# A fused attention and two-MoE kernel on one core: another place for the short token block, and low parts on VectorE

## The chip, the cores and the metric

The kernel runs on one core of one Trainium2 chip. The metric is the device time of one execution in microseconds (us). TensorE is called PE here, VectorE DVE, ScalarE ACT, GpSimd POOL; PEld is the weight load that stands ahead of each matmul, and SP is the engine that issues the DMAs.

## What is computed

Multi-head attention with a threshold under the row maximum, then two dense two-layer stages ("MoE" and "MoE 2"), all in float32. The change touches the second one alone (`_moe2_ref`):

```python
x = np.ascontiguousarray(attn_out.transpose(0, 2, 1, 3)).reshape(B * S, H * D)   # 2304 x 512
x = _moe_ref(x=x, **moe_kwargs)

def _moe2_ref(x, w_in, w_out):        # x 2304 x 512, w_in 512 x 2048, w_out 2048 x 512
    h = x @ w_in
    g = h * (1.0 / (1.0 + np.exp(-1.702 * h)))
    return g @ w_out
```

## The kernel before, in words

**Split products.** Every factor of a product is kept as a high and a low part (fp32r). The high part is a rounding copy made by ACT; the low part is source minus high part, a two-input subtraction on DVE or POOL. A product is three matmuls: high x high, high x low, low x high.

**The second MoE** walks over the tokens in blocks: four full ones of 512 tokens (first tokens 0, 512, 1024, 1536) and a short one of 256 (first token 2048; `BLOCKS`, L351). It does so twice, once for each half of the 2048 hidden units, eight units of 128 columns in a half, taken in four pairs. The first pass stores its result to DRAM (`y2d`), the second adds to it and writes the output. Before, the first pass goes short, 0, 512, 1024, 1536, and the second 0, 512, 1024, 1536, short.

**A block** (`moe2`, L922) has three steps. `halves` (L814) loads the block's inputs in two halves of the model dimension (tiles xa and xb, one buffer each) and makes the left factors from them: seven for a full block, which multiplies two-by-two blocks with seven products instead of eight, and two for the short block. A full block needs four subtractions first (xt, xa, xb written; called XD here). Each factor i is then a copy on ACT (outhring, called XHC) and a subtraction of 128 x 512 (outlring, called XLC) on the engine `XENG[i]` (L353): before, POOL for factors 0, 2, 4 and 6, DVE for 1, 3 and 5. The factors live in a ring of eight buffers. `hidden2` (L871) makes the hidden values of a pair: seven products (six matmuls of 256 columns each) for a full block, four for a short one, with ACT copies (p, u, c) and DVE additions (c) that take results out of PSUM, four banks (pm) in all. `gate2` (L858) applies the gate to each unit of the pair: a sigmoid on ACT (tc), a product on DVE (tc), the high part on ACT (g) and the low part (g, called GL here) on the engine that `hidden2` hands it: before, POOL for the first unit of a pair and DVE for the second, and DVE for both in a block's last pair. `yout` then multiplies both units into four accumulators (py): 24 matmuls of 512 columns for a pair of a full block, of 256 for the short one.

**Beside the first blocks** other work runs on the same engines: the int64-coded weights of the last pair of the first half are decoded, and those of the second half, which are stored (kept) for the second pass. A decode is ACT, DVE and POOL work on tiles wrstg, wmstg and ws, and high and low parts inhring, inlring, outhring, outlring (ring1) again.

**What sets the order.** Nothing is written in program order: a planner places every operation by a due time and a table of costs, and each engine then runs its own list in that order. So an operation that waits holds back all that stands behind it on its engine. The tiles xa and xb live in memory that the first MoE's inputs hold (`change2`, L1016), so the first loads of the second MoE go out only after the last hidden product of the first.

Of the kernel before, what the change touches and what calls it, by code (L numbers as in the profile page):

```python
# [21 lines left out]
PE, ACT, DVE, POOL, SP, DMA = range(6)  # L22
# [220 lines left out]
def tile_top_attention_moe_moe2(  # L243
# [52 lines left out]
    def add(eng, cost, time, name, fn, rd=(), wr=(), touch=()):  # L296
        op = pl.add(eng, cost, time, fn, rd, wr, name, touch)
        for c, names in zip(changed, (LATE, LAST)):
            if any(b.pool in names for b in op.bufs):
                op.deps.add(c)  # L300
        return op
# [14 lines left out]
    def mark():  # L316
        return Buf(pl, "mark", 1 << 30, None, "")
# [12 lines left out]
    def act(n):  # L330
        return 51 + 0.834 * n
# [18 lines left out]
    x1d_b, ypd_b, x2d_b = ({(b, p): mark() for b in range(B) for p in range(2)} for _ in range(3))  # L350
    BLOCKS = [(NT - NT % 512, NT % 512)] + [(c, 512) for c in range(0, NT - 511, 512)]  # L351
    y2d_b = {c: mark() for c, _ in BLOCKS}
    XENG = (POOL, DVE, POOL, DVE, POOL, DVE, POOL)  # L353


    id_b, id2_b, two_b = const("id", [P, P]), const("id2", [P, 64]), const("two", [P, P])
# [457 lines left out]
    def halves(c0, n, whole, K):  # L814
# [15 lines left out]
        def put(i, src, rd):  # L830
# [5 lines left out]
            add(ACT, 93 + act(2 * n), K("XHC") + i, "XHC", copy(lambda: v(h), src), rd, [h])  # L836
            eng = XENG[i]
            add(eng, pool2(2 * n) if eng == POOL else dve(2 * n), K("XLC") + i, "XLC", tt(eng, lambda: v(l), src, lambda: f32(v(h)), ALU.subtract), rd + [h], [l])
# [32 lines left out]
    def hidden2(n, w, xs, whole, K, engs):  # L871

        a, b = (buf("c", 3, "ct", [P, 512]) for _ in range(2))
        p1 = buf("p1", 1, "ct", [P, 256])
        ba, bd = (bank(3) for _ in range(2))
        T = n if whole else 2 * n

        def mm(o, wi, xi, st, sp):
            (wh, wl), k0 = w[wi]
            xh, xl = xs[xi]  # L880
            for kk in range(2):
                ws, xv = slice(k0 + kk * P, k0 + kk * P + P), slice(kk * n, kk * n + n)
                for i, (u, v) in enumerate(((wh, xh), (wh, xl), (wl, xh))):
                    nc.tensor.matmul(o.t[:, :n], u.t[:, ws], v.t[:, xv], start=(st and kk == 0 and i == 0), stop=(sp and kk == 1 and i == 2), skip_group_check=True)  # L884

        def prod(o, wi, xi, st, sp):
            add(PE, 6 * pe(n), K("H2") + 640 * xi, "H", lambda: mm(o, wi, xi, st, sp), [*w[wi][0], *xs[xi]], [o, line] if st else [o])

        def first(x):
            return lambda: x.t[:, :n]  # L890

        def second(x):
            return lambda: x.t[:, n:2 * n]

        def plus(t, o, x, y, reg):
            add(DVE, dve(n), K("H2") + 4000, "U", tt(DVE, o, first(x), first(y), ALU.add), [x, y], [(t, reg)])

        prod(ba, 0, 0, True, False)
        add(ACT, act(n), K("H2") + 1000, "KP", copy(first(p1), first(ba)), [ba], [p1])
        if whole:  # L900
            prod(ba, 1, 1, False, True)
            add(ACT, act(n), K("H2") + 3000, "KP", copy(first(a), first(ba)), [ba], [a])
            prod(bd, 6, 0, True, False)
            prod(bd, 3, 1, False, True)
            plus(b, first(b), bd, p1, 0)
            return [gate2(c, T, K, eng) for c, eng in zip((a, b), engs)]
        p5, u2, bb = buf("p5", 1, "ct", [P, 256]), buf("u2", 1, "ct", [P, 256]), bank(3)
        prod(bd, 4, 1, True, False)
        add(ACT, act(n), K("H2") + 1700, "KP", copy(first(p5), first(bd)), [bd], [p5])
        prod(bb, 1, 2, True, True)  # L910
        plus(a, first(a), bb, p1, 0)
        prod(ba, 5, 3, False, False)
        add(ACT, act(n), K("H2") + 3000, "KP", copy(first(u2), first(ba)), [ba], [u2])
        prod(bd, 2, 4, False, True)
        plus(a, second(a), bd, u2, 1)
        prod(ba, 6, 5, False, False)
        plus(b, second(b), ba, p5, 1)
        prod(ba, 3, 6, False, True)
        add(ACT, act(n), K("H2") + 5000, "KP", copy(first(b), first(ba)), [ba], [(b, 0)])
        return [gate2(c, T, K, eng) for c, eng in zip((a, b), engs)]  # L920

    def moe2(c0, T, f0, w, t0, last):  # L922

        whole, n = T < 512, min(T, 256)
        dt = 19.2 * T

        def K(name, i=0):
            return t0 + dt * i + NOMINAL[name]

        xs = halves(c0, n, whole, K)  # L930
        pys = [buf(f"py{c}", 1, "py", [P, 512]) for c in range(KC)]

        def yout(i, gs):
            for j, (gh, gl) in enumerate(gs):
                wo = wt[1, "out", f0 + 2 * i + j]
                for c in range(KC):
                    add(PE, 3 * pe(T), K("Y", i + 1), "Y", lambda c=c, gh=gh, gl=gl, wo=wo, st=i + j == 0, sp=i + j == len(w):
                        out_mm(pys[c], T, wo, gh.t[:, :T], gl.t[:, :T], c, st, sp), [*wo, gh, gl], [pys[c]] if c else [pys[c], line])

        gs = None  # L940
        for i in range(len(w)):
            g2 = hidden2(n, w[i], xs, whole, lambda name, i=i: K(name, i), (DVE, DVE) if i == len(w) - 1 else (POOL, DVE))
            if i:
                yout(i - 1, gs)
            gs = g2
        yout(len(w) - 1, gs)
        for c in range(KC):
            yc = buf("yc", 5, "yc", [P, 512])
            t = K("YO", len(w) + 1)

            def o(yc=yc):
                return yc.t[:, :T]

            def y(c=c):
                return pys[c].t[:, :T]

            rows = slice(c * P, (c + 1) * P)
            if last:
                move(K("LP"), "LP", 4 * P * T, lambda o=o, rows=rows: nc.sync.dma_start(out=o(), in_=y2d[rows, c0:c0 + T]), [y2d_b[c0]], [yc])
                add(DVE, dve(T), t, "YO", tt(DVE, o, y, o, ALU.add), [pys[c]], [yc])  # L960
            elif c % 2:
                add(ACT, act(T), t, "YO", copy(o, y), [pys[c]], [yc])
            else:
                add(DVE, dve(T), t, "YO", lambda o=o, y=y: nc.vector.tensor_copy(out=o(), in_=y()), [pys[c]], [yc])
            move(t, "SO", 4 * P * T, lambda o=o, rows=rows: nc.sync.dma_start(out=(out if last else y2d)[rows, c0:c0 + T], in_=o()), [yc], [] if last else [y2d_b[c0]])
# [44 lines left out]
    w = [pair(f, t + 30000 * f // 2) for f in range(0, HF // 2, 2)]  # L1010
# [5 lines left out]
    changed.append(add(SP, 0, 0, "change", change2))  # L1016
    changed[1].deps |= {o for o in pl.ops if any(x.pool in MIDDLE for x in o.bufs)}
    for half in range(2):
        for c0, n in BLOCKS[half:] + BLOCKS[:half]:
            moe2(c0, n, half * HF, w, t, half == 1)  # L1020
            t += 19.2 * n * len(w)
        if half == 0:
            w = [fetch_pair(HF + f, kept[f // 2], t - 30000 + 4800 * f) for f in range(0, HF, 2)]
# [56 lines left out]
```

## Time and profile before

| | us |
|---|---|
| median of 3 runs | 1129.56 (1124.95 to 1130.73) |
| the profiled execution: time | 1127.03 |
| the profiled execution: span, first to last instruction | 1125.2 |
| PE busy | 1091.7 (97%) |
| DVE busy | 797.0 (71%) |
| ACT busy | 703.6 (63%) |
| POOL busy | 640.5 (57%) |

The second MoE begins in this execution at 722.6 us, with the first matmul on an outhring tile, and lasts to the end. The granted TensorE clock is 1.00 there from its first stretch to the last. A busy PE is read with care, since matmuls are pipelined and overlap in the records; a weight load stands ahead of each matmul, so that the idle time ahead of a weight load shows by how much the matmul behind it came late.

### The profile page before, as it was taken

What the parts mean: (1) busy time and instruction counts of PE and PEld (TensorE: products, weight loads), DVE (VectorE), ACT (ScalarE), POOL (GpSimd) and SP (SyncE); (2) the same over time, 40 slices, a digit from 0 to 9 for tenths busy, and PEclk for the clock granted to TensorE, in tenths of its full rate; (3) what the DMA queues carried; (4) which work ended last, traced back from release to release, by engine and by line L of the source; (5) the groups of instructions that cost most, each with busy time, mean ns of one, the idle gap of its engine ahead of it and who ended that gap; (6) DMA issues with size and microseconds to landing.
All of it is one profiled execution on the core that took longest, in us unless ns stands there. A gap on an engine that the chain in (4) does not pass through costs nothing.

```text
span 1125.2 us, 21023 instructions
## 1 busy us (share of the span) xinstructions
PE 1091.7 (97%) x7560; PEld 1005.3 (89%) x7560; DVE 797.0 (71%) x1654; ACT 703.6 (63%) x1444; POOL 640.5 (57%) x684
## 2 busy tenths in 40 slices
PE   7999999999999999999999999988999999999998
PEld 4566899999999999999999999987889889889888
DVE  7888885999699959687876432697877665644633
ACT  5888886888588867666554323665555664543533
POOL 5788896989598966466466223674443453321300
PEclk9999999999999999999999999999999999999999
DMA  6444121322123210245654312434435344312202
GB/s 186 135 137 144 62 79 39 103 78 76 46 79 87 91 36 29 83 137 161 202 182 131 97 55 69 160 106 162 155 124 186 120 129 136 113 38 75 90 1 71
DMA packets 78985, 117.83 MB, mean 105 GB/s; under 512 B 7713, under 2 KB 50081, under 8 KB 78881
## 3 DMA queue, kind: packets, MB, share of 16 engines
q1 hardware_dynamic: 78880, 116.49, 33.0%
q8 instruction: 60, 0.98, 0.4%
q14 instruction: 45, 0.36, 0.1%
HBM read 85.92 MB, written 30.54 MB: 103 GB/s over the span
## 4 chain that ended last, share of the span: by engine, by line
PE 68%; DVE 14%; ACT 6%; POOL 4%; DMA 4%; issue 4%; SPq 1%; POOLq 0%; DVEq 0%; ACTq 0%
PE py L747 19%; PE pm L727 14%; PE pm L884 12%; PE pm L747 7%; PE pm L599 4%; PE ps L539 4%; PE pm L662 3%; DVE e L551 2%; DVE nm L548 2%; PE pm L664 2%; PE pm L666 1%; DVE el L346 1%; DVE g L346 1%; PE ps L535 1%; DVE tc L346 1%
## 5 line engine op out<-in xcount | busy, mean ns | idle before, releaser
L747 PE MATMUL py<-g,outhring 128*128 128x512 f32 (+2 forms) x1152 | 290.1, 338 | 9.8 <-DVE g L346 6.0
L747 PEld LDWEIGHTS py<-g,outhring 128*128 128x128 f32 x1152 | 194.8, 189 | 31.5 <-DVE g L346 10.5
L747 PE MATMUL py<-g,outlring 128*128 128x512 f32 (+2 forms) x576 | 193.7, 336 | 0.0
L727 PE MATMUL pm<-xh,inhring 128*128 128x256 f32 (+1 forms) x512 | 153.6, 300 | 0.5 <-DVE el L346 0.2
L727 PE MATMUL pm<-xl,inhring 128*128 128x256 f32 (+1 forms) x512 | 151.5, 296 | 0.0
L727 PE MATMUL pm<-xh,inlring 128*128 128x256 f32 (+1 forms) x512 | 151.4, 296 | 0.0
L884 PE MATMUL pm<-outhring,inhring 128*128 128x256 f32 x512 | 144.8, 283 | 5.4 <-DVE c L346 3.0
L884 PE MATMUL pm<-outlring,inhring 128*128 128x256 f32 x512 | 143.8, 281 | 0.0
L884 PE MATMUL pm<-outhring,inlring 128*128 128x256 f32 x512 | 143.7, 281 | 0.0
L346 POOL TENSOR_TENSOR g<-t,g 128x256 fp32r<-128x256 f32 (+1 forms) x104 | 86.3, 832 | 93.4 <-ACT g L343 90.5
L739 DVE SCALAR_TENSOR_TENSOR t<-t,pm 128x256 f32<-128x256 f32 (+1 forms) x128 | 57.4, 450 | 92.5 <-ACT t L738 92.0
L343 ACT ACTIVATE eh<-pm 128x512 fp32r<-128x512 f32 (+9 forms) x240 | 108.2, 487 | 21.5 <-PE pm L599 20.0
L346 POOL TENSOR_TENSOR g<-tc,g 128x512 fp32r<-128x512 f32 (+1 forms) x30 | 39.5, 1316 | 140.8 <-ACT g L343 89.5
L548 DVE TENSOR_REDUCE nm<-ps 128x1 f32<-128x576 f32 x144 | 107.5, 752 | 16.9 <-PE ps L539 10.2
L747 PEld LDWEIGHTS py<-g,outlring 128*128 128x128 f32 x576 | 108.5, 188 | 9.7
L747 PE MATMUL pm<-g,outhring 128*128 128x256 f32 (+1 forms) x512 | 110.1, 304 | 0.3
L550 ACT ACTIVATE e<-ps,nm 128x576 f32<-128x576 f32 x128 | 93.6, 739 | 24.4 <-DVE nm L548 22.2
L738 ACT ACTIVATE t<-pm,half 128x256 f32<-128x256 f32 (+1 forms) x128 | 63.7, 497 | 72.0 <-PE pm L727 66.9
L551 DVE SCALAR_TENSOR_TENSOR e<-ps,th,e 128x576 f32<-128x576 f32 x128 | 102.8, 812 | 6.3 <-ACT e L550 4.1
L884 PEld LDWEIGHTS pm<-outhring,inhring 128*128 128x128 f32 x512 | 96.8, 189 | 9.8 <-DVE c L346 4.1
L346 POOL TENSOR_TENSOR wmstg<-wmstg,wrstg 128x512 uint32<-128x512 uint32 x48 | 66.2, 1380 | 61.3 <-DVE wmstg L399 36.8
L727 PEld LDWEIGHTS pm<-xh,inhring 128*128 128x128 f32 x512 | 96.9, 189 | 2.6 <-PE pm L599 0.7
(122 smaller groups left out, 2888.5 us busy)
## 6 DMA issues: line engine op xcount, KB each, us to landing
wrawstg<-in_w1i_dram SPq DMA_DIRECT2D x16, 512.0 KB, 3.8
wrawstg<-in_w1o_dram SPq DMA_DIRECT2D x16, 512.0 KB, 3.5
wrawstg<-in_w2i_dram SPq DMA_DIRECT2D x16, 512.0 KB, 4.0
wrawstg<-in_w2o_dram SPq DMA_DIRECT2D x16, 512.0 KB, 3.7
qk<-in_k_dram SPq DMA_DIRECT2D x28, 288.0 KB, 3.0
qk<-in_q_dram SPq DMA_DIRECT2D x26, 288.0 KB, 3.0
wrawstg<-kept SPq DMA_DIRECT2D x20, 256.0 KB, 2.9
xa<-x2d SPq DMA_DIRECT2D x8, 512.0 KB, 3.6
```

Of the source, the lines that this page charges most:

```text
L343: return lambda: nc.scalar.activation(out=o(), in_=i(), func=ACTF.Copy, **kw)
L346: return lambda: (nc.vector if eng == DVE else nc.gpsimd).tensor_tensor(out=o(), in0=a(), in1=b(), op=op)
L539: nc.tensor.matmul(ps.t[:, i, :SH], qs[hd].t[:, q0:q0 + P], w[hd].t[:, i * SH:(i + 1) * SH], start=a, stop=z)
L548: add(DVE, 665, K("R", s), "R", lambda: nc.vector.tensor_reduce(out=nm.t[:, c], in_=ps.t[:, :, :SH], op=ALU.max, axis=AX.XY, negate=True), ...
L550: add(ACT, 624, K("X", s), "X", lambda: nc.scalar.activation(out=ev(), in_=ps.t[:, :, :SH], func=ACTF.Exp, bias=nm.t[:, c]), [ps, (nm, s)] ...
L551: add(DVE, 729, K("M", s), "M", lambda: nc.vector.scalar_tensor_tensor(out=ev(), in0=ps.t[:, :, :SH], scalar=th.t[:, c], in1=ev(), op0=ALU ...
L599: nc.tensor.transpose(pt.t[:kn, o + m * P:o + (m + 1) * P], e_of[s].t[:, ks], id_b.t)
L727: nc.tensor.matmul(ph.t[:, :n], a, v, start=(cc == 0 and i == 0), stop=(cc == KC - 1 and i == 2))
L738: add(ACT, 93 + act(n), K("RL"), "RL", lambda: nc.scalar.activation(out=tt_(), in_=pt(), func=ACTF.Relu, scale=1.0 / 6.0, bias=half_b.t), ...
L739: add(DVE, dve(n), K("GT"), "GT", lambda: nc.vector.scalar_tensor_tensor(out=tt_(), in0=tt_(), scalar=1.0, in1=pt(), op0=ALU.min, op1=ALU. ...
L747: nc.tensor.matmul(py.t[:, :n], a, v, start=(st and i == 0), stop=(sp and i == 2))
L884: nc.tensor.matmul(o.t[:, :n], u.t[:, ws], v.t[:, xv], start=(st and kk == 0 and i == 0), stop=(sp and kk == 1 and i == 2), skip_group_che ...
```

## The change

Three edits. In the first pass the short block goes second, behind block 0, instead of first; the second pass is as before. All low parts of the blocks' inputs (XLC) are put on DVE: 4 more of each full block's seven and 1 more of the short block's two. In short blocks the low part of the gated units (GL) is on DVE for every pair. Over the whole program 40 instructions go from POOL to DVE: 34 of 128 x 512 and 6 of 128 x 256. What PE computes is the same.

```diff
-    XENG = (POOL, DVE, POOL, DVE, POOL, DVE, POOL)
+    XENG = (DVE,) * 7
@@ moe2
-            g2 = hidden2(n, w[i], xs, whole, lambda name, i=i: K(name, i), (DVE, DVE) if i == len(w) - 1 else (POOL, DVE))
+            g2 = hidden2(n, w[i], xs, whole, lambda name, i=i: K(name, i), (DVE, DVE) if whole or i == len(w) - 1 else (POOL, DVE))
@@ the two passes
     for half in range(2):
-        for c0, n in BLOCKS[half:] + BLOCKS[:half]:
+        for c0, n in [x for y in ([BLOCKS[1:2], BLOCKS[:1], BLOCKS[2:]], [BLOCKS[1:], BLOCKS[:1]])[half] for x in y]:
             moe2(c0, n, half * HF, w, t, half == 1)
```

The planner places everything again. Up to the last units of the first MoE the lists of all engines read alike; from there on they differ. Numbers behind a name tell buffers apart.

DVE before, where the second MoE begins: behind the subtraction for the short block's second factor (xb) stand the last sums of the first MoE (yc), and block 0's first XD (xt) comes between a decode's steps (ws, wmstg) and the short block's gates:

```order
L346 TENSOR_TENSOR outlring2_10008<-xb_9957,outhring2_9992 128x512
L346 TENSOR_TENSOR yc_9570<-py0_9769,yc_9570 128x320
L346 TENSOR_TENSOR yc_9702<-py1_9775,yc_9702 128x320
L346 TENSOR_TENSOR yc_9760<-py2_9783,yc_9760 128x320
L346 TENSOR_TENSOR yc_9791<-py3_9787,yc_9791 128x320
L346 TENSOR_TENSOR xt_10068<-xa_10010 128x512
L346 TENSOR_TENSOR ws_10081<-wmstg2_9935 128x256
L346 TENSOR_TENSOR tc_10070<-tc_10070,c_10058 128x256
```

DVE after, at the same place: nine subtractions for block 0's factors (XD and XLC) stand in one row, ahead of those sums.

```order
L346 TENSOR_TENSOR xt_9998<-xa_9950 128x512
L346 TENSOR_TENSOR outlring2_10008<-xa_9950,outhring2_9990 128x512
L346 TENSOR_TENSOR xt_10016<-xb_9955,xt_9998 128x512
L346 TENSOR_TENSOR outlring2_10023<-xb_9955,outhring2_10011 128x512
L346 TENSOR_TENSOR outlring2_10022<-xt_9998,outhring2_10010 128x512
L346 TENSOR_TENSOR xa_9950<-xa_9950,xb_9955 128x2x256
L346 TENSOR_TENSOR outlring2_10052<-xt_10016,outhring2_10028 128x512
L346 TENSOR_TENSOR outlring2_10063<-xb_9955,outhring2_10029 128x512
L346 TENSOR_TENSOR outlring2_10073<-xa_9950,outhring2_10054 128x512
L346 TENSOR_TENSOR c_10084<-pm_10056,p1_10050 128x256
L346 TENSOR_TENSOR yc_9570<-py0_9769,yc_9570 128x320
```

What moved: block 0's whole preparation now stands where the short block's single subtraction stood.

POOL before, while the short block's last pairs are gated: the low parts of block 0's factors (from xa and xb) stand between the steps of the last pair's weights (wmstg, outlring1):

```order
L346 TENSOR_TENSOR g_10282<-tc_10234,g_10259 128x256
L346 TENSOR_TENSOR outlring2_10174<-xa_10010,outhring2_10060 128x512
L346 TENSOR_TENSOR wmstg2_10268<-wmstg2_10268,wrstg2_10320 128x512
L346 TENSOR_TENSOR outlring1_10370<-wmstg2_10251,outhring1_10323 128x512
L346 TENSOR_TENSOR outlring1_10374<-wmstg2_10268,outhring1_10366 128x512
L346 TENSOR_TENSOR outlring2_10207<-xb_10024,outhring2_10110 128x512
L346 TENSOR_TENSOR outlring2_10219<-xb_10024,outhring2_10121 128x512
```

POOL after, while the last pairs of block 0 are gated: the same weights, with a gate between them.

```order
L346 TENSOR_TENSOR wmstg2_10300<-wmstg2_10300,wrstg2_10214 128x512
L346 TENSOR_TENSOR outlring1_10358<-wmstg2_10300,outhring1_10341 128x512
L346 TENSOR_TENSOR g_10380<-tc_10335,g_10356 128x512
L346 TENSOR_TENSOR wmstg2_10312<-wmstg2_10312,wrstg2_10347 128x512
L346 TENSOR_TENSOR outlring1_10450<-wmstg2_10312,outhring1_10438 128x512
```

What moved: no low part of an input is left in POOL's list.

DVE before, in the second pass where one full block ends and the next is prepared:

```order
L346 TENSOR_TENSOR outlring2_12794<-xt_12423,outhring2_12782 128x512
L346 TENSOR_TENSOR c_12804<-pm_12784,p1_12770 128x256
L346 TENSOR_TENSOR tc_12802<-tc_12802,c_12759 128x512
L346 TENSOR_TENSOR outlring2_12824<-xt_12497,outhring2_12813 128x512
L346 TENSOR_TENSOR xb_12442<-xb_12442,xt_12497 128x2x256
L346 TENSOR_TENSOR g_12838<-tc_12802,g_12826 128x512
```

DVE after, at the same place:

```order
L346 TENSOR_TENSOR outlring2_12794<-xt_12444,outhring2_12782 128x512
L346 TENSOR_TENSOR c_12804<-pm_12784,p1_12770 128x256
L346 TENSOR_TENSOR outlring2_12809<-xb_12415,outhring2_12792 128x512
L346 TENSOR_TENSOR tc_12802<-tc_12802,c_12759 128x512
L346 TENSOR_TENSOR outlring2_12824<-xt_12470,outhring2_12813 128x512
L346 TENSOR_TENSOR outlring2_12828<-xb_12415,outhring2_12819 128x512
L346 TENSOR_TENSOR g_12833<-tc_12802,g_12826 128x512
L346 TENSOR_TENSOR xb_12415<-xb_12415,xt_12470 128x2x256
```

What moved: two low parts that were POOL's stand ahead of the gate's low part (g), and the XD that writes xb has gone behind it.

## Rows read from the trace of the kernel before

**Rows 1.** Stretches: busy us (instructions) of PE, PEld, DVE, ACT, POOL; clock, DMA.
```profile
722.50:799.70 77.20, 68.00 (x464) 61.89 (x463) 63.35 (x100) 47.04 (x99) 43.91 (x31) 1.00 0.44 141
799.70:935.00 135.30, 132.17 (x836) 118.57 (x835) 98.79 (x157) 83.75 (x167) 59.30 (x41) 1.00 0.47 155
935.00:1055.00 120.00, 119.55 (x741) 106.21 (x740) 65.09 (x101) 57.37 (x117) 33.01 (x23) 1.00 0.23 73
```
**Rows 2.** Whom the weight loads waited for, 722.5 to 799.7: total us, times, longest.
```profile
PEld py L747 <- POOL g L346: 3.2, 3, 1.6
PEld py L747 <- DVE g L346: 3.1, 2, 1.9
PEld pm L884 <- DVE c L346: 2.4, 2, 1.4
PEld pm L884 <- ACT p L343: 1.7, 2, 1.5
PEld pm L884 <- ACT u L343: 1.2, 1, 1.2
```
**Rows 3.** The same view from 799.7 to 1125.
```profile
PEld py L747 <- DVE g L346: 5.5, 10, 1.4
PEld pm L884 <- DVE c L346: 1.7, 2, 1.0
PEld py L747 <- POOL g L346: 0.5, 1, 0.5
```
**Rows 4.** PE in order of time: start, us, line, tiles, [idle before <- releaser].
```profile
722.56 0.28 PE L884 MATMUL pm<-outhring,inhring 128*128 128x256 f32 x1
...
747.85 0.39 PE L747 MATMUL py<-g,outhring 128*128 128x256 f32 x1 [1.71 <-DVE g L346]
```
**Rows 5.** DVE in order of time ahead of 747.85.
```profile
746.31 2.92 DVE L346 TENSOR_TENSOR g<-tc,g 128x256 fp32r<-128x256 f32 x2
```
**Rows 6.** POOL in order of time, the same stretch.
```profile
746.05 2.90 POOL L346 TENSOR_TENSOR outlring<-wmstg,outhring 128x512 fp32r<-128x512 f32 x2
```
**Rows 7.** DVE groups by shape, 722.5 to 799.7: xcount | busy us, mean ns | idle.
```profile
L346 DVE TENSOR_TENSOR g<-tc,g 128x256 fp32r<-128x256 f32 x5 | 5.3, 1071 | 0.2 <-ACT g L343 0.2
...
L346 DVE TENSOR_TENSOR outlring<-xa,outhring 128x512 fp32r<-128x512 f32 x2 | 1.9, 925 | 0.0
```
**Rows 8.** One DVE group of the same view, 850 to 1125.
```profile
L346 DVE TENSOR_TENSOR g<-tc,g 128x256 fp32r<-128x256 f32 x5 | 2.0, 420 | 0.3 <-ACT g L343 0.2
```
**Rows 9.** One POOL group by shape, 722.5 to 799.7.
```profile
L346 POOL TENSOR_TENSOR outlring<-xb,outhring 128x512 fp32r<-128x512 f32 x6 | 9.2, 1542 | 9.3 <-ACT outhring L343 9.3
```
**Rows 10.** Instructions on tile xa: xcount, ns minimum/median/maximum.
```profile
L346 POOL TENSOR_TENSOR outlring<-xa,outhring x10: 1309/1748/1757, 720.3 to 1052.9; 128x512 fp32r<-128x512 f32 x10
...
L346 DVE TENSOR_TENSOR outlring<-xa,outhring x8: 675/678/1170, 735.5 to 1048.6; 128x512 fp32r<-128x512 f32 x8
```
**Rows 11.** SP in order of time: the first load of the second MoE.
```profile
716.60 0.37 SPq L820 DMA_DIRECT2D xa<-x2d  x1
```
**Rows 12.** DMAs issued from 716 to 727: count, KB each, us to landing.
```profile
xa<-x2d SPq DMA_DIRECT2D x1, 512.0 KB, 4.0
xb<-x2d SPq DMA_DIRECT2D x1, 512.0 KB, 4.7
```
**Rows 13.** ACT in order of time: ahead of the second MoE's first sigmoid.
```profile
726.28 1.28 ACT L865 ACT_TABLE_LOAD   x1
```
**Rows 14.** DVE in order of time where a full block ends in the second pass.
```profile
957.86 0.70 DVE L346 TENSOR_TENSOR outlring<-xt,outhring 128x512 fp32r<-128x512 f32 x1 [1.55 <-ACT outhring L343]
...
959.17 1.38 DVE L346 TENSOR_TENSOR tc<-tc,c 128x512 f32<-128x512 f32 x1 [0.28 <-ACT tc L865]
960.47 0.68 DVE L346 TENSOR_TENSOR outlring<-xt,outhring 128x512 fp32r<-128x512 f32 x1
961.08 1.79 DVE L346 TENSOR_TENSOR xb<-xb,xt 128x512 f32<-128x512 f32 x1
962.79 0.68 DVE L346 TENSOR_TENSOR g<-tc,g 128x512 fp32r<-128x512 f32 x1
```

## The prediction

> **What bounds the kernel now.** Read the stretches first [rows 1]. PE is busy 119.55 of 120 us in the second pass (935 to 1055): there nothing but less PE work would help, and the change computes the same. The exception is where the second MoE begins: from 722.5 to 799.7 us PE is busy 68.0 of 77.2, with DVE at 63.35 and POOL at 43.91. This stretch is the short block and block 0, both orders' first two blocks. So the question is which waits stand there, and whether the change moves what ends last.
>
> Then the waits of the weight loads, which tell how late each matmul came [rows 2]: 3.2 + 3.1 + 2.4 + 1.7 + 1.2 = 11.6 us in ten waits, for low parts of gates (g) from POOL and DVE, for sums (c) from DVE and for PSUM copies (p, u) from ACT. From 799.7 to the end it is 5.5 + 1.7 + 0.5 = 7.7 us in thirteen [rows 3]. More than 19.3 us can't be won.
>
> Why g is late is seen at the longest wait [rows 4]: the matmul at 747.85 waits for DVE's g. DVE's two g from 746.31 take 2.92 us, 1.46 each [rows 5], where the same form takes 0.42 late in the kernel [rows 8]; POOL runs one subtraction after the other in that time [rows 6], 1.45 us each. So a DVE instruction with both operands in SBUF comes through about once per POOL instruction. Over the stretch this form has a mean of 1.07 us [rows 7]. Twelve groups of DVE are longer there than alone (0.42 us for 256 columns, 0.68 for 512 [rows 8, 10]), from the first group of rows 7, 5 x (1.071 - 0.420) = 3.3 us, to the last, 2 x (0.925 - 0.678) = 0.5; together 17 us of DVE's 63. POOL's burst there holds low parts of block 0's inputs, which are not urgent, between weights that are.
>
> The Trainium skill (SBUF — State Buffer, Who interferes with whom) says that a DVE instruction with two SBUF inputs and a GpSimd instruction that reads SBUF exclude each other, and that whichever started first keeps the other out for its whole length. By that rule the moved subtractions can be kept out themselves, which speaks against the change; rows 5 and 6 agree with it.
>
> **XLC and GL on DVE.** In the stretch 9 low parts of 128 x 512 and 3 of 128 x 256 change engine. On POOL one of 512 columns takes 1.31 us at least and 1.54 in the stretch [rows 9, 10]; on DVE 0.68, and 0.61 from start to start in a row of such [rows 10, 14]. DVE gets 9 x 0.61 + 3 x 0.35 = 6.5 us more work. POOL issues 18 instead of 31 instructions, so of the 17 us that DVE loses to POOL 13/31, or 7.1 us, go. DVE's total stays where it is (63 us), and POOL's falls by some 17 us. This is no gain by itself: it is that the urgent steps on both engines meet fewer others.
>
> **The short block goes second.** One pair of the short block is 24 matmuls of 256 columns and four products, about half a full block's PE work, but the same number of gates and the same weights to be decoded. First in line, it asks for the last pair's weights and gates in half the time. Behind block 0 these are ready: by the lists, the last pair's weights are decoded before PE asks for them some 40 us into the second MoE. What it costs is the start: seven factors and four XD instead of two factors.
>
> Walk that start with the rows. The first load goes out at 716.6 [rows 11], as before, for it waits for the first MoE's last hidden product. Twice as large now (512 KB each), the loads land after 4.0 and 4.7 us [rows 12]: xa at 720.6, xb at 721.7. PE begins the first product at 722.6 now [rows 4]; it has two sums of the first MoE left then, 0.9 us, and these come first in the new list, so it asks for factor 0 at 723.4 and for a next one every 0.7 us. DVE's nine subtractions in a row take 9 x 0.61 = 5.5 us from 720.6: 726.1, or 727.1 with one POOL instruction in the way. Factor 5, the last of them, is asked for at 727.6: no wait. Factor 6 stands behind two sums, four yc and an XD, and comes at about 731.1, where PE asks at 730.3: 0.8 us. Then the load of ACT's table, 1.28 us [rows 13], stands behind factor 6's copy: the first sigmoid ends at about 732.0, a PSUM copy (u) behind it makes PE wait 0.4 us, and the first gate's low part, on POOL, comes at 735.3 where PE asks at 734.3: 1.0 us. Together 2.2 us.
>
> In the short block, now second, I find three places where its low part on DVE stands behind another pair's sum (c) or factor: 0.3 + 0.3 + 0.4 = 1.0 us. With 0.4 us for what the walk misses, 3.6 us are left of 11.6: **gain 8.0 us**. Bounds: every one of the eleven preparing subtractions could meet POOL (each 0.5 us longer, 1.17 us against 0.68 [rows 10]), which makes the start 2.2 + 5.5 = 7.7 us and the gain 2.5; at best nothing waits but 1.0 us, gain 10.6.
>
> **The rest of the kernel.** At a full block's end DVE holds up PE (ten waits for g [rows 3]). One such place [rows 14]: from 957.86 to the end of g at 963.47, a gate's product takes 1.38 and an XD 1.79 us, each beside a POOL low part; ten waits of this kind make 5.5 us, 0.55 in the mean. In the new list two more XLC stand ahead of g, the XD behind it. With nothing on POOL: 0.61 + 0.35 + 0.61 + 0.61 + 0.61 + 0.61 + 0.68 = 4.1 us, so g ends at 961.9, 1.5 us sooner, and a wait of 0.55 us is gone. If half of all such waits, and those in decoding from 799.7 to 860, are left, 2 us are won for sure enough to be taken: between 0 (the XLC take back what POOL gives) and 5. PE work, DMA volume and the last block are as before: 0.
>
> **Sum.** 8.0 + 2.0 = 10 us off. The profiled execution had 1127.0, 2.5 under the median of the runs (1129.56); off the median it gives 1119.6, taken as 1120.
>
> **Rivals.** *DVE takes the place of the waits (within 0.5%).* DVE was busy 63 of 77 us and keeps these 63 us in a stretch of 69: nine tenths. If its list holds back sums and copies as POOL did g, the start costs 7.7 us, the rest gives nothing, and the gain is about 3: 1126.5. For it: the nine subtractions stand ahead of every sum and gate, and c from DVE made PE wait already [rows 2, 3]. Against it: PE asks for these factors one by one, at 0.7 us each, and DVE makes one, XD included, in about 0.95 with three us of lead.
>
> *All waits of this kind go.* 10.6 + 5 = 15 us: 1114.5. For it: the longest waits have POOL in them [rows 4 to 6]. Against it: the table load and ACT's copies are not touched.
>
> *Slower: low parts ahead of gates at every full block's end.* Eight full blocks get four more XLC, 2.4 us each. If POOL's remaining gates and weights keep DVE out as long as now, this stands fully ahead of g at seven block ends: 17 us, less 8: 1139. It outweighs the start's gain from 1.2 us per block end. Against it: in the list two of the four stand ahead of g, and POOL has almost nothing left there in the second pass.
>
> *That the change doesn't do what it says* is ruled out by the lists: 40 instructions have changed engine, and PE's work is the same in another order.
>
> **Chances.** Forecast (1116 to 1123) 0.55; all waits go 0.12; DVE takes their place (1124 to 1131) 0.27; slower 0.06. About 0.5%, 5.6 us, is what a measurement of this kernel can tell from no change; the forecast's own size lies above it, so faster 0.70, same 0.24, slower 0.06. The range leaves out the slower case and half of the ends: 1114.5 to 1127.
>
> **What would show it.** Right: from 722.5 us the first two blocks end some 8 us sooner, their waits add up to 3 or 4 us, among them one behind the table load; DVE's g of 256 columns has a mean near 0.5 us instead of 1.07; the second pass shows hardly a wait for g. Wrong: waits for DVE's low parts of inputs (outlring) among PE's, ahead of the first products or at block ends, or DVE busy without a gap through the first 70 us. Wrong by size: the same PE idle time elsewhere, from 799.7 on.

## The result and the profile after

The changed kernel takes **1114.76 us** (median of 4 runs, 1114.12 to 1116.56), the kernel before in the same comparison 1129.68 (1124.95 to 1130.73). The ratio is 0.9871 with a 95% interval of 0.9845 to 0.9898: 14.9 us faster. The profiled execution took 1114.85 us, with a span of 1112.8; before it was 1127.03 and 1125.2. Between the two profiled executions lie 12.2 us.

The stretches that answer to [rows 1], in the same columns; the first now ends at 791, where the short block and block 0 are done:

```profile
722.50:791.00 68.50, 66.30 (x458) 60.98 (x457) 58.40 (x106) 44.54 (x95) 24.18 (x17) 1.00 0.45 140
791.00:935.00 144.00, 143.12 (x914) 129.03 (x913) 105.40 (x183) 90.32 (x184) 46.84 (x34) 1.00 0.49 161
935.00:1055.00 120.00, 119.63 (x757) 107.38 (x756) 65.30 (x116) 55.66 (x115) 10.41 (x9) 1.00 0.23 77
```

The two blocks' PE work (68.0 and 66.3 us busy) now fits into 68.5 us instead of 77.2. POOL has 24.18 us of work in the stretch instead of 43.91. DVE has taken over subtractions and yet is busy 58.40 instead of 63.35; some of block 0's now run ahead of 722.5, as the rows of DVE further down show.

The waits of the weight loads, 722.5 to 791, which answer to [rows 2] (total us, times, longest):

```profile
PEld pm L884 <- DVE c L346: 1.1, 2, 0.9
PEld py L747 <- DVE g L346: 0.9, 2, 0.7
PEld pm L884 <- ACT u L343: 0.6, 1, 0.6
PEld py L747 <- ACT g L343: 0.6, 1, 0.6
PEld pm L884 <- DVE outlring L346: 0.4, 1, 0.4
```

And from 791 to the end, for [rows 3]:

```profile
PEld py L747 <- DVE g L346: 2.1, 5, 0.5
PEld py L747 <- POOL g L346: 1.2, 1, 1.2
PEld pm L884 <- DVE c L346: 0.6, 2, 0.4
PEld py L747 <- ACT g L343: 0.2, 1, 0.2
```

So 11.6 us of waits became 3.6, and 7.7 became 4.1: 11.6 us of the 12.2 between the profiled executions are in these two lists. The rest lies ahead of the change: the last matmul of the first MoE's hidden products started at 715.39 instead of 716.26 us.

DVE's low part of a gate, 256 columns wide, from 722.5 to 799.7, for [rows 7] (count, busy us, mean ns, idle). Its mean was 1071 ns:

```profile
L346 DVE TENSOR_TENSOR g<-tc,g 128x256 fp32r<-128x256 f32 x8 | 3.5, 467 | 0.1
```

### The profile page after: what moved, and what is told of

It is laid out like the page before. It is cut to its first block, busy times and chain, and to the rows that moved or that the text cites. A ratio compares the mean times of both kernels' runs of the same rounds, so it can differ in the third digit from the quotient of the medians.

```text
span 1112.8 us, 20973 instructions
## 1 busy us (share of the span) xinstructions
PE 1089.5 (98%) x7560; PEld 1006.0 (90%) x7560; DVE 793.1 (71%) x1694; ACT 701.9 (63%) x1444; POOL 579.6 (52%) x644
## 4 chain that ended last, share of the span: by engine, by line
PE 77%; DVE 11%; ACT 4%; POOL 3%; issue 3%; DMA 2%; SPq 0%; DVEq 0%; POOLq 0%; ACTq 0%
PE py L747 24%; PE pm L727 15%; PE pm L884 14%; PE pm L747 7%; PE pm L599 4%; PE ps L539 4%; PE pm L662 3%; DVE e L551 2%; DVE nm L548 2%; PE pm L664 2%; PE ps L535 2%; PE pm L666 1%; DVE el L346 1%; DMA wrawstg<-kept 1%; ACT eh L343 1%
## 5 line engine op out<-in xcount | busy, mean ns | idle before, releaser
L346 POOL TENSOR_TENSOR g<-tc,g 128x512 fp32r<-128x512 f32 x24 | 33.2, 1382 | 164.7 <-ACT g L343 156.0
L884 PEld LDWEIGHTS pm<-outlring,inhring 128*128 128x128 f32 x512 | 97.0, 189 | 3.0 <-DVE outlring L346 0.4
## 6 DMA issues: line engine op xcount, KB each, us to landing
wrawstg<-kept SPq DMA_DIRECT2D x20, 256.0 KB, 2.9
```

The costliest lines, as they stand in the source:

```text
L346: return lambda: (nc.vector if eng == DVE else nc.gpsimd).tensor_tensor(out=o(), in0=a(), in1=b(), op=op)
```

## Experiments

Each kernel was compared with the kernel before on the same chip. What is stated of waits below is worked out from the trace. For every matmul, from the last one of the first MoE's hidden products on, I take the time from the start of the one ahead of it and subtract what that step takes when nothing waits (0.114 us for 256 columns, 0.147 for 320, 0.229 for 512). Steps over by more than 0.06 us are summed as **delay**. The **length** runs from the start of that matmul to the end of the last one, so it leaves out nearly all of the first MoE. The last column is the time in stretches where the granted clock was 0.50 (the 1.2 GHz level), whose slower steps are in the delay too.

| kernel | short block | low parts on DVE | ratio (95%) | length us | delay: first two blocks / rest of pass 1 / pass 2 | at 0.50 |
|---|---|---|---|---|---|---|
| before | first | as before | 1 | 405.8 | 11.9 / 4.6 / 2.0 | 0 |
| before, again (e11) | first | as before | | 407.4 | 12.9 / 5.2 / 2.1 | 0 |
| e2 | first | inputs | 0.9973 (0.9952–0.9994) | 402.8 | 10.6 / 2.7 / 2.1 | 3.4 |
| e3 | first | inputs, short gates | 0.9939 (0.9918–0.9960) | 401.3 | 11.2 / 0.7 / 2.5 | 10.2 |
| e12 | first | inputs, all gates | 0.9941 (0.9923–0.9959) | 400.4 | 11.5 / 1.6 / 0 | 10.2 |
| e1 | second | as before | 1.0013 (0.9993–1.0034) | 410.1 | 15.6 / 3.7 / 2.1 | 6.8 |
| e4 | second | inputs | 0.9922 (0.9896–0.9948) | 396.8 | 8.5 / 0.7 / 1.4 | 3.4 |
| after | second | inputs, short gates | 0.9871 (0.9845–0.9898) | 393.9 | 4.2 / 0.4 / 2.6 | 0 |
| after, again (e5) | second | inputs, short gates | 0.9883 (0.9863–0.9903) | 393.6 | 3.0 / 0.7 / 2.2 | 0 |
| e10 | second | inputs, all gates | 0.9857 (0.9836–0.9879) | 391.6 | 3.4 / 0.7 / 0.3 | 0 |
| e7 | second | inputs of the first two blocks, short gates | 0.9932 (0.9916–0.9948) | 400.3 | 6.3 / 3.6 / 2.4 | 0 |
| e8 | second | as after, table loaded early | 0.9901 (0.9885–0.9918) | 394.6 | 4.4 / 1.2 / 1.4 | 0 |
| e6 | second | as after, POOL reads again | 0.9987 (0.9969–1.0004) | 407.2 | 9.8 / 3.5 / 6.1 | 10.2 |
| e9 | second | as after, POOL writes instead | 0.9914 (0.9897–0.9930) | 401.6 | 9.2 / 1.7 / 4.0 | 6.8 |

Length less delay is 386 to 388.5 us in all fourteen profiles. The waits, with the slower clock behind some of them, are nearly the whole difference.

### The parts alone

The prediction put nearly all of its gain on the short block's place and said of the move of low parts "this is no gain by itself". e1 makes only the first, e2 only the other for the inputs, e3 both moves to DVE without the order, e4 the order and the inputs' low parts without the gates.

e1, order only:

```diff
-    XENG = (DVE,) * 7
+    XENG = (POOL, DVE, POOL, DVE, POOL, DVE, POOL)
...
-(DVE, DVE) if whole or i == len(w) - 1 else (POOL, DVE))
+(DVE, DVE) if i == len(w) - 1 else (POOL, DVE))
```

(Here and below the diff is against the changed kernel, and of a long line only the end stands here where the rest is the same.)

> The kernel before with one edit alone: the short block goes second in the first pass; low parts stay where they were. Theory of the place (the short block first asks for the last pair's weights and gates too early): most of the gain of the whole change, 7 to 10 us of 15, and the waits of the first two blocks fall from 12 to 4 to 6 us. Theory of the port (POOL's low parts keep DVE's instructions out, wherever the short block stands): at most 3 us, and 8 us or more of waits stay in the first two blocks, since the same 31 POOL instructions run there.

Measured: 1.0013 (0.9993 to 1.0034), no gain, so the place alone is not it. PE's waits from 722.5 to 800:

```profile
PEld pm L884 <- ACT p L343: 2.7, 2, 1.7
PEld py L747 <- ACT g L343: 2.1, 1, 2.1
PEld pm L884 <- ACT u L343: 2.0, 1, 2.0
PEld py L747 <- POOL g L346: 1.5, 1, 1.5
PEld py L747 <- DVE g L346: 1.0, 1, 1.0
PEld pm L884 <- DVE outlring L346: 0.9, 1, 0.9
```

10.2 us where the kernel before had 11.6, and of other kinds: with block 0 first, its seven factors and the ACT copies queued behind them stand on the path, and POOL makes four of the factors, one per 1.3 to 1.7 us. On top of it the clock fell twice behind such waits. PE around the first (start, us, ..., idle before):

```profile
737.92 0.39 PE L884 MATMUL pm<-outhring,inhring 128*128 128x256 f32 x1 [1.82 <-ACT u L343]
...
739.14 0.42 PE L884 MATMUL pm<-outlring,inhring 128*128 128x256 f32 x1
739.36 0.41 PE L884 MATMUL pm<-outhring,inlring 128*128 128x256 f32 x1
...
742.13 0.28 PE L884 MATMUL pm<-outhring,inhring 128*128 128x256 f32 x1
742.25 0.28 PE L884 MATMUL pm<-outlring,inhring 128*128 128x256 f32 x1
```

The stretch between, in the columns of [rows 1]:

```profile
738.70:742.10 3.40, 3.40 (x17) 3.34 (x16) 1.22 (x4) 2.43 (x6) 2.39 (x2) 0.50 0.78 249
```

The matmuls come every 0.21 us in between instead of every 0.11, at a granted clock of 0.50. A stretch of 3.4 us costs up to 1.7.

e2, low parts of the inputs only:

```diff
-(DVE, DVE) if whole or i == len(w) - 1 else (POOL, DVE))
+(DVE, DVE) if i == len(w) - 1 else (POOL, DVE))
...
-        for c0, n in [x for y in ([BLOCKS[1:2], BLOCKS[:1], BLOCKS[2:]], [BLOCKS[1:], BLOCKS[:1]])[half] for x in y]:
+        for c0, n in BLOCKS[half:] + BLOCKS[:half]:
```

> The kernel before with one edit alone: all low parts of the blocks' inputs on DVE, the short block first. Theory of the place: 2 to 5 us faster, the waits around the short block's last pairs stay (6 us or more in the first two blocks). Theory of the port: 9 us or more, DVE's low part of a gate of 256 columns falls from a mean of 1.07 us to below 0.6 in the first two blocks.

Measured: 0.9973 (0.9952 to 0.9994), some 3 us: the size that the theory of the place had, a third of what the theory of the port had.

e3, low parts and gates, in the old order:

```diff
-        for c0, n in [x for y in ([BLOCKS[1:2], BLOCKS[:1], BLOCKS[2:]], [BLOCKS[1:], BLOCKS[:1]])[half] for x in y]:
+        for c0, n in BLOCKS[half:] + BLOCKS[:half]:
```

> The whole change without its order: low parts of inputs and of the short block's gates on DVE, the short block first. Theory of the place: 3 to 7 us faster, so 8 us or more of the change are lost with the order. Theory of the port: within 3 us of the whole change's 15.

Measured: 0.9939 (0.9918 to 0.9960). Its longest waits from 722.5 to 800:

```profile
PEld py L747 <- ACT g L343: 2.4, 1, 2.4
PEld py L747 <- POOL outlring L346: 2.2, 1, 2.2
PEld py L747 <- ACT outhring L343: 0.8, 1, 0.8
```

The first is for the first pair's gate. The second and third are waits for the last pair's weights, which the short block asks for before POOL and ACT have decoded them. This is what the prediction said of the old order. It stands out now that the conflicts are fewer.

e4, order and low parts of the inputs, without the gates:

```diff
-(DVE, DVE) if whole or i == len(w) - 1 else (POOL, DVE))
+(DVE, DVE) if i == len(w) - 1 else (POOL, DVE))
```

> The whole change without its smallest part: the low parts of the short block's gates stay on POOL for the first unit of a pair. Theory of the place and theory of the port alike expect at most 1 us less than the whole change (13.5 to 15 us faster), as three subtractions of 256 columns in each pass are all that is moved.

Measured: 0.9922 (0.9896 to 0.9948). With the six gates of 256 columns left on POOL the length is 3.0 us more than the changed kernel's (396.8 against the mean of its two profiles, 393.8). This is more than the 1 us expected, but by the ratios not clear of noise: the interval meets those of both measurements of the changed kernel. One wait at the short block's end and the slow stretch behind it make most of that. It is for a gate on DVE, whose product (tc) met a decode step on POOL; how the six gates bring it about is not shown. PE in order of time:

```profile
798.33 0.40 PE L747 MATMUL py<-g,outhring 128*128 128x256 f32 x1 [1.85 <-DVE g L346]
```

The stretch behind it:

```profile
798.60:802.00 3.40, 3.40 (x18) 3.40 (x18) 1.41 (x5) 0.00 (x0) 0.00 (x0) 0.50 0.02 8
```

So no part alone is worth the whole. By length, against the mean of the two profiles of before (406.6): the order alone loses 3.5 us, the two moves alone win 5.3, all together win 12.9 (393.75, the mean of after's two).

### The changed kernel and the kernel before once more

> The changed kernel itself, timed again beside the three that follow, since the runs so far show the first MoE, whose lists are the same in every kernel, ending between 715.4 and 722.9 us. If the median of four runs was not favoured by that spread, 13.5 to 16 us faster than before; if it was, 11 to 13.5, which is what the second MoE alone got shorter in the profile (11.9 us).

> The kernel before, profiled a second time: is the length of its second MoE (405.8 us from the first MoE's last hidden product to the last matmul, 18.6 of it waits) typical? Expected 404 to 410, with the waits of the first two blocks at 10 to 14 us; if a stretch of lower clock falls into it, 1.7 us more for each.

e5 is the changed kernel unedited: 0.9883 (0.9863 to 0.9903), 13.1 us less than the 1131.80 of before on that chip. By its expectation the 14.9 us of the result were helped by the spread of the first MoE's end; the lengths give 12.9. e11, before unedited, took 1130.67 us in its one execution. Their lengths repeat within 0.3 and 1.6 us.

### Is it the conflict on SBUF, or POOL's time?

Two theories explain why taking work from POOL helps. By the first, a POOL instruction that reads SBUF holds up DVE's instructions with two SBUF inputs. By the second, only POOL's list got shorter, so what is urgent on it comes sooner. e6 leaves the changed kernel's work as it is and gives POOL its reading back: 34 subtractions of 128 x 512 whose result nobody uses.

```diff
+            if i % 2 == 0:
+                d = buf("dm", 1, "xs", [P, 512], F32)
+                add(POOL, pool2(2 * n), K("XLC") + i, "XLC", lambda: nc.gpsimd.tensor_tensor(out=d.t[:, :2 * n], in0=f32(h.t)[:, :2 * n], in1=f32(h.t)[:, :2 * n], op=ALU.subtract), [h], [d])
```

> The changed kernel, and POOL does a subtraction of 128 x 512 again for each low part that it lost (it reads the factor's high part twice and writes a tile that nobody reads; the output is the reference's). DVE's work stays the changed kernel's, POOL's load is that of the kernel before. Theory of the port: the gain goes, within 5 us of the kernel before. Theory of the chain (with block 0 first PE asks for a factor every 0.7 us, which DVE can give and POOL can't): at least 9 us of the gain stay.

Measured: 0.9987 (0.9969 to 1.0004): the gain is gone. But e6 also makes POOL's list longer. e9 has the same lists on PE, DVE, ACT and SP, in the same order, and at the same places on POOL a subtraction of one column and three writes of 128 x 512 in the subtraction's place:

```diff
+            if i % 2 == 0:
+                d = buf("dm", 1, "xs", [P, 512], F32)
+
+                def fill():
+                    nc.gpsimd.tensor_tensor(out=d.t[:, :1], in0=f32(h.t)[:, :1], in1=f32(h.t)[:, :1], op=ALU.subtract)
+                    for _ in range(3):
+                        nc.gpsimd.memset(d.t, 0.0)
+
+                add(POOL, pool2(2 * n), K("XLC") + i, "XLC", fill, [h], [d])
```

> The same lists as the kernel with POOL's load given back (e6), word for word on PE, DVE, ACT and SP; on POOL each added subtraction is replaced by one of a single column, which waits for the same factor, and three memsets of 128 x 512, which keep POOL busy about as long but read nothing. Theory of the port (what keeps DVE out is POOL's reading of SBUF beside DVE's two inputs): at least 6 us of the 12 that e6 lost come back, so 8 us or more faster than before, and DVE's instructions of two inputs get their short times. Theory of POOL's list (gates and weights come late because they stand behind other POOL work, whatever it does): no more than 3 us come back.

Measured: 0.9914 (0.9897 to 0.9930). What was added on POOL in e6 (a POOL group by shape, as [rows 9]):

```profile
L841 POOL TENSOR_TENSOR dm<-outhring 128x512 f32<-128x512 f32 x34 | 42.7, 1257 | 38.4 <-ACT outhring L343 35.1 <-PE py L747 2.9
```

The whole stretch from 722.5 to 1120 in e6, in the columns of [rows 1]:

```profile
722.50:1120.00 397.50, 386.62 (x2474) 350.88 (x2472) 264.98 (x445) 210.64 (x437) 127.00 (x96) 0.99 0.35 112
```

What was added in e9:

```profile
L845 POOL MEMSET dm<- 128x512 f32 x102 | 54.8, 537 | 5.9
L843 POOL TENSOR_TENSOR dm<-outhring 128x1 f32<-128x1 f32 x34 | 14.2, 419 | 22.5 <-ACT outhring L343 21.8
```

The stretch in e9:

```profile
722.50:1120.00 397.50, 389.49 (x2520) 354.96 (x2519) 258.61 (x452) 211.96 (x442) 153.16 (x198) 0.99 0.35 112
```

And in the changed kernel, which has neither:

```profile
722.50:1120.00 397.50, 383.39 (x2498) 347.97 (x2496) 250.94 (x449) 209.84 (x437) 84.02 (x61) 1.00 0.34 111
```

The added work is longer in e9 (54.8 + 14.2 = 69.0 us against 42.7) and POOL is busier (153 against 127 us), yet e9 is faster by 0.73% of the time before, 8 of the 12 to 13 us that e6 lost, and by 5.6 us in length; DVE is busy 6.4 us less in it, and 9.0 less over the whole length. With POOL's time alone as the cause, e9 had to be the slower one. So reading on POOL costs time here, and writing costs less. The Trainium skill (SBUF — State Buffer, Who interferes with whom) says so: a DVE instruction with two SBUF inputs contends with a GpSimd instruction that reads SBUF, not with one that only writes it. e9's trace agrees: its DVE instructions of this kind, 128 x 512 wide, took 683 ns in the mean where they met nothing but memsets (33 of them), 687 where POOL was idle (107), and 987 where they met another POOL instruction (37).

The trace of the kernel before shows the form of the conflict. From 715 us on, DVE's 28 instructions of this kind and width that began ahead of the POOL instruction they met took 0.68 to 0.69 us. The 41 that began while a POOL instruction of 128 x 512 was running, with 0.15 us or more of it left, ended 0.55 us behind its end, 1.80 us long at most. However early they began, their end hangs on POOL's, as if DVE stood still until then.

That is not the whole: e9 is 7.8 us longer than the changed kernel (401.6 against 393.8). Its lists differ from the changed kernel's, since the planner places 34 more POOL steps, and each still reads a column; PE waits for ACT's copies (p, 1.8 and 2.0 us) where it did not, and the clock fell behind each of these waits. Between these causes the runs don't decide.

### Where the low parts are moved

e7 moves the inputs' low parts to DVE in the first two blocks only, 5 of 34, with the gates as in the change:

```diff
-            eng = XENG[i]
+            eng = XENG[i] if on_dve else (POOL, DVE, POOL, DVE, POOL, DVE, POOL)[i]
...
-        xs = halves(c0, n, whole, K)
+        xs = halves(c0, n, whole, K, not last and c0 in (0, 2048))
```

> The changed kernel, but the low parts of inputs are on DVE alone in the first pass's first two blocks (block 0 and the short one); all later blocks have them on POOL and DVE by turns, as before. Theory of the chain: within 4 us of the changed kernel, as the start is where a factor ends last. Theory of the port: half or less of the gain, 7 us or less, since 29 of 34 moved instructions are back on POOL.

Measured: 0.9932 (0.9916 to 0.9948), about half the gain, and so between what the two theories said. Against the means of before, 12.4 and 4.9 us, it wins 6.1 us of delay in the first two blocks and 1.3 in the rest of pass 1. The other 29 are worth another 6.5 us of length (400.3 to 393.8), of which 2.7 are still in the first two blocks' stretch, since the next block is prepared there too.

### The table load at the start

e8 has ACT load its table ahead of the second MoE, by one sigmoid of one column placed earlier:

```diff
+    pre = buf("pre", 1, "xs", [P, 1])
+    add(ACT, 1340, t - 3000, "PRE", lambda: nc.scalar.activation(out=pre.t, in_=half_b.t, func=ACTF.Sigmoid), [half_b], [pre])
```

> The changed kernel with one more ACT instruction: a sigmoid of one column, placed before the last high part of the first MoE, so that ACT's table is loaded ahead of the second MoE's first copies. By the trace the three waits behind the load (0.5, 0.8 us and one of 0.4) should shrink: 1 to 2 us faster than the changed kernel. If POOL's low part of the first gate ends last anyway, less than 0.5 us.

Measured: 0.9901 (0.9885 to 0.9918), no better than the changed kernel. The wait for u behind the load is gone, but DVE's g and c are waited for in its place (2.2 and 0.9 us of the 4.3 from 722.5 to 800):

```profile
PEld py L747 <- DVE g L346: 2.2, 4, 1.1
PEld py L747 <- ACT g L343: 1.0, 3, 0.5
PEld pm L884 <- DVE c L346: 0.9, 1, 0.9
...
```

There was little to win: in the first 25 us of the length the delay is 1.4 us in e8, 2.4 in the first profile of the changed kernel and 1.3 in its second, which has the load where it was. The rest of the first two blocks has 3.1 us instead of 1.8 in both; that other chains, ending close behind, then show is the likely reading, not a tested one.

### Going on: all gates on DVE

e10 puts the low parts of the full blocks' gates on DVE as well:

```diff
-(DVE, DVE) if whole or i == len(w) - 1 else (POOL, DVE))
+(DVE, DVE))
```

> The changed kernel, with the low parts of all gates of the second MoE on DVE, which leaves POOL the weights alone. Theory of the port: what is left of waits (6 to 7 us) falls further, 1 to 3 us faster than the changed kernel. Rival, DVE as the new bound: DVE gets 29 more subtractions of 0.61 us, and sums and gates come later; 0 to 3 us slower.

Measured: 0.9857 (0.9836 to 0.9879), 1116.54 us against 1133.20: the fastest version by ratio, though its interval overlaps that of the changed kernel. Its second pass runs without a gap, with POOL idle (same columns):

```profile
935.00:1055.00 120.00, 120.00 (x749) 108.42 (x749) 69.31 (x121) 52.93 (x111) 0.00 (x0) 1.00 0.23 74
```

e12 is e10 with the short block first again:

```diff
-(DVE, DVE) if whole or i == len(w) - 1 else (POOL, DVE))
+(DVE, DVE))
...
-        for c0, n in [x for y in ([BLOCKS[1:2], BLOCKS[:1], BLOCKS[2:]], [BLOCKS[1:], BLOCKS[:1]])[half] for x in y]:
+        for c0, n in BLOCKS[half:] + BLOCKS[:half]:
```

> The kernel of e10 (low parts of inputs and of all gates on DVE, POOL left with the weights alone) with the old order: the short block first in both of the first pass's places. Does the order matter once POOL's list is short? Theory of the place (the short block first asks for the last pair's weights before they are decoded): 5 us or more slower than e10, so 8 to 12 us faster than before, with two or three waits of 2 us on the last pair's weights and gates. Theory of the port alone: within 3 us of e10.

Measured: 0.9941 (0.9923 to 0.9959). The waits from 722.5 to 800:

```profile
PEld py L747 <- ACT g L343: 2.2, 1, 2.2
PEld py L747 <- POOL outlring L346: 2.2, 1, 2.2
...
```

These are e3's waits with POOL emptier still. The second is for the last pair's weights: in the old order this pair comes too early for them, however little POOL has to do. The first is for the first pair's gate, which ACT makes behind its table load and two copies of block 0. PE in order of time:

```profile
731.17 0.84 PE L747 MATMUL py<-g,outhring 128*128 128x256 f32 x2 [2.03 <-ACT g L343]
```

By its expectation e12 is as much slower than e10 as the theory of the place said (9.5 us by the ratios, 5 or more expected), though it wins 7 us over the kernel before and not 8 to 12. The order's worth therefore grows with the move to DVE: in ratio 0.0013 lost with the old engines, then 0.005 won (e2, e4), 0.006 (e3 with after and e5) and 0.008 (e12, e10).

## Why the prediction was right, and where it was not

The forecast was 1120 us, faster; it is 1114.76, in the range by 0.3 us.

**The first two blocks: right.** 8.0 us were forecast and 11.6 - 3.6 = 8.0 measured. By the delay, which holds the restarts too, it is 11.9 - 4.2 = 7.7. The walk gave 2.2 us at the start; the delay there is 2.4. Its pieces were less exact. DVE's nine subtractions started at 719.48, not 720.6; 0.9 of this is the earlier end of the first MoE. Two of the nine met POOL, the first and the eighth, as the Trainium skill's rule in the prediction allowed (DVE in order of time):

```profile
719.48 0.96 DVE L346 TENSOR_TENSOR xt<-xa 128x512 f32<-128x512 f32 x1 [0.73 <-DMA xa<-x2d]
...
723.38 0.68 DVE L346 TENSOR_TENSOR outlring<-xt,outhring 128x512 fp32r<-128x512 f32 x1
723.98 1.78 DVE L346 TENSOR_TENSOR outlring<-xb,outhring 128x512 fp32r<-128x512 f32 x1
```

and POOL beside it:

```profile
718.42 1.47 POOL L346 TENSOR_TENSOR wmstg<-wmstg,wrstg 128x512 uint32<-128x512 uint32 x1
...
723.59 1.62 POOL L346 TENSOR_TENSOR inlring<-wmstg,inhring 128x512 fp32r<-128x512 f32 x1 [3.69 <-PE pm L884]
```

PE then waited 0.5 us for factor 6 (0.8 forecast) and 0.6 for u behind the table load (0.4). The third wait was not the gate's 1.0 us but one for a sum, and the gate was there in time behind it (PE):

```profile
730.20 0.39 PE L884 MATMUL pm<-outlring,inhring 128*128 128x256 f32 x1 [0.25 <-DVE outlring L346]
...
731.42 0.39 PE L884 MATMUL pm<-outhring,inhring 128*128 128x256 f32 x1 [0.37 <-ACT u L343]
...
733.74 0.38 PE L884 MATMUL pm<-outhring,inhring 128*128 128x256 f32 x1 [0.68 <-DVE c L346]
```

The idle time that PE's rows show is shorter than the delay (0.25 for 0.5), since the matmul ahead is still draining. The short block's waits, in three places, cost 1.8 us of delay with the restarts behind them (772.6, 773.0, 785.2), 1.5 by the weight loads, instead of 1.0. That the waits left met the forecast 3.6 us to a tenth is in part luck: the same view has 2.6 us in e5.

**"DVE's total stays where it is": wrong, though the loss was sized right.** The step took from DVE's 17 us of loss to POOL the share of POOL's instructions that go, 13/31, or 7.1 us, against 6.5 us of added work (the instructions that move are 12 of the 31). Counted in the trace (each DVE instruction against the median of its form beside an idle POOL), the loss fell from 17.0 us to 9.3, by 7.7. Two of the twelve groups in it are one-input decoding steps (wmstg from wmstg, 0.42 us alone at 512 columns), so POOL holds up more than instructions with two inputs; in e9 such a step beside memsets took up to 0.76 us. That DVE's total fell further, from 63.35 to 58.40, is not loss saved: the stretch holds six other DVE instructions less (106 in all, where 100 and the 12 moved would be 112), and those in a row overlap more. Over the whole second MoE, where the other work is the same, DVE got 40 instructions more, 25 us by their time alone, and was busy 256.0 us instead of 260.6; its loss fell from 47.3 to 21.7 us.

**"This is no gain by itself", and the order's 8 us: wrong.** This is the step that failed in its reasons, though the sum held. e3 wins 0.6% without the order, and e1 nothing with it alone. The parts need each other: behind block 0, the last pair's weights are in time, but the start then needs block 0's factors quickly, and with POOL making four of them PE's delay in the first 25 us is 5.8 us (e1, a slow stretch in it) instead of 2.4.

**The rest: right in sign, too small, and in another place.** 2.0 us were forecast, 7.7 - 4.1 = 3.6 measured. The step named the full blocks' ends in the second pass, where "a wait of 0.55 us is gone". At the gate that [rows 14] showed, it is: this g stands at 949.08 now instead of 962.79, and PE, which comes to it at 950.87, runs through. But the next gate, the last pair's first, is late. The rows of both; first DVE:

```profile
949.08 0.68 DVE L346 TENSOR_TENSOR g<-tc,g 128x512 fp32r<-128x512 f32 x1
...
951.41 0.68 DVE L346 TENSOR_TENSOR outlring<-xa,outhring 128x512 fp32r<-128x512 f32 x1
952.01 0.69 DVE L346 TENSOR_TENSOR outlring<-xb,outhring 128x512 fp32r<-128x512 f32 x1
952.61 0.69 DVE L346 TENSOR_TENSOR tc<-tc,c 128x512 f32<-128x512 f32 x1
954.10 0.69 DVE L346 TENSOR_TENSOR g<-tc,g 128x512 fp32r<-128x512 f32 x1 [0.81 <-ACT g L343]
```

and PE:

```profile
950.87 0.63 PE L747 MATMUL py<-g,outhring 128*128 128x512 f32 x2
...
954.33 1.02 PE L747 MATMUL py<-g,outhring 128*128 128x512 f32 x2
955.19 0.40 PE L747 MATMUL py<-g,outlring 128*128 128x512 f32 x1
```

The last pair's first gate stands behind two low parts (outlring), a product (tc) and ACT, and holds up PE by 0.4 us (two matmuls in 1.02 instead of 0.62), where it cost 0.1 before, in all three such places of the pass. In the whole pass the weight loads' waits for DVE's g went only from 2.6 to 1.6 us, and one for POOL's g, 1.2 us at 932 in the pass's first block, is new. So the second pass won nothing, and the sign that it would show hardly a wait for g did not come. What was won lies in the first pass: in the decoding from 799.7 to 860, which the step only mentioned, from 1.7 + 1.4 + 0.5 = 3.6 us to 0.2.

**The rest of the difference.** By the profiled executions the gain is 12.2 us where 10 were forecast. The medians are 14.9 apart because before's profiled execution lay 2.5 us under its median, as the prediction said, and the changed kernel's on it.

**The rivals.** DVE did not take the waits' place: one wait for an input's low part is among them, of 0.4 us by the weight loads. Low parts ahead of a gate cost 0.3 us at three block ends, and the gate before them won as much. That all waits go gave 1114.5, close to the median, but 7.7 us of waits are left.

## What to carry to other kernels

Where two engines hold each other up, count both engines' stretched instructions before saying that moving work to the busier one costs anything: DVE got 25 us more work over the second MoE and was busy 4.6 us less. Two changes that each win little can need each other, so make each with and without the other before naming a cause; the order was worth from -0.1% to 0.8%, by what else was done. Compare the stretch that the change touches, not the whole span, when another part varies by as much as the gain.

## What the runs showed of the hardware

- **A slower clock behind long waits.** In seven of the profiled kernels the granted clock fell to 0.50 (1.2 GHz) in the second MoE for 3.4 us, or 6.8, around the end of delays of 1.8 to 2.7 us of PE: e1 behind an idle time of 1.82, e4 behind 1.85, e6 in its second pass too (the row below). A stretch of 3.4 us costs up to 1.7 us on top of the wait. Delays of 1.4 to 1.9 us in the kernel before brought none in two profiles; why, these runs don't tell.

```profile
932.70:939.50 6.80, 6.19 (x29) 6.20 (x30) 4.52 (x8) 3.44 (x8) 2.25 (x2) 0.50 0.67 238
```

- **POOL's writes.** A memset of 128 x 512 on POOL takes 0.54 us, and a subtraction of 128 x 1 still 0.42 (e9's rows above).
- **The first MoE does not end at the same time twice.** Its lists are the same in all these kernels nearly to its end, but the last matmul of its hidden products started between 715.39 and 722.90 us in fourteen profiles. Eight of the profiles show a granted clock of 0.50 for 3.4 us near 550 us, but the earliest of the fourteen (after) is among them and the second latest (e5) is not; the source of the spread is open. It is why e4's span (1122.9) is no shorter than e3's (1122.2), although its length is 4.5 us shorter.
